# Joins and residuals as accumulating transfers, and two more quarters of attention output by block products

## The chip, the cores and the metric

The kernel runs on one core of a Trainium2 chip. The metric is the device time of one execution in microseconds. TensorE (PE in the profile) multiplies matrices into PSUM. VectorE (DVE), ScalarE (ACT) and GpSimd (POOL) work on SBUF, and DVE and ACT read PSUM too. SyncE (SP) issues most transfers; POOL issues those that add to what is at their destination. Every engine works through its own instructions in the order in which they were written and waits on semaphores.

## The reference

`x` is 2048 tokens of 512 numbers. After a layer norm it goes through attention with 32 heads over a cache of 2048 keys, and through a mixing MLP; the MLP's output, passed through a SiLU, gates the attention's output, and `x` is added.

```python
x = A_x                                           # [1, 2048, 512]
xn = _layernorm(x, axis=-1)
q = (xn @ wq) -> [1, 32, 2048, 128]
p = softmax(q @ k_cache^T * Dh ** -0.5)
s = (p @ v_cache) -> [1, 2048, 4096] @ wo          # attention
g = _silu(_B_ref(xn, w1, w2, w3, w4))              # gate
return x + s * g
```

## The kernel before, in words

**Units and slots.** The 32 heads form eight groups of four (`g` from 0 to 7). The 2048 queries form four quarters of 512 (`qt` from 0 to 3). One head on one quarter is a unit: 128 units, unit number `(g * 4 + qt) * 4 + hh`. A unit takes eight slots of 256 keys. In each slot TensorE makes scores for 256 keys (two matmuls into `ps_s`, L443), ACT takes their exponential (L447), and TensorE multiplies exponentials of ten slots earlier with the values (`ps_o`, L480). The main loop (L1152) writes all other work of all engines into these slots, so its order is fixed by hand: a table `todo` (`at(n, fn)`) and two tables `o_steps` and `o_early` say what is issued in which slot. A slot's number is eight times the unit plus `p`.

**Sums of exponentials.** DVE adds the first two pieces of exponentials (L453) and then the rest; half of one of these adds goes to POOL (`add_half`, L458, at `p == 6`), and DVE's own half and the next add (L462) follow at the start of the next unit. Two folds (L466, L470), a transposing transfer, a reduction (L500), a reciprocal (L506) and two small transfers make the row of factors `rb` with which DVE scales the unit's output into `oT` (L524).

**Queries.** The queries of two heads at a time come from seven block products instead of eight (`product`, L378); DVE puts the pieces together (L424 to L434) just ahead of the unit that needs them. The last of these is L432.

**Output projection.** A quarter of a group, four heads, is multiplied with four heads' rows of `wo`, into `sacc`, one float accumulator per 128 tokens `t` (16 of them). In the plain form (`wo_slot`, `wo_mm`) each `t` takes four matmuls of 512 columns into the bank `xm`, and DVE adds the bank to `sacc` (L668). In the block form (the list `BLOCK`) pairs of token tiles take seven products of two matmuls of 256 columns (`wo_product`, L576), with operand sums on DVE (`wo_sum` L564, `o_sum` L573), and DVE adds partial sums to a tile `sp[qt, i]` of five columns of 256 (`wo_take`, L598). The columns 0 and 2 of it belong to one token tile, 1 and 4 to another, and column 3 holds what has to be added to columns 1, 2 and 4 once, after all groups: this is `wo_join` (L604). The plain quarters of group 7 are then added to the same columns.

**The end.** Token tiles 0 to 7 get their last plain product and are then scaled by half the gate and get `x` added (`y_last`, L674), with `x` and the gate loaded by `fin_load`. For token tiles 8 to 15 (`LATE`) the scaling of `sacc` (`y_scale`, L636) and the addition of `x` (`y_add`, L640, an accumulating transfer that POOL issues) are done ahead of the last product, with the gate loaded by `gate_load` (L607) into buffers that the block form has no more use for. The marker `LATER` (L1109) is the first unit of the quarter behind the last block quarter; joins, scalings and the plan `PLAN` for taking up plain work again are placed relative to it.

Of the kernel before, what the change touches and what calls it, by code (L numbers as in the profile page):

```python
# [9 lines left out]
ALU = mybir.AluOpType  # L10
FP32 = mybir.dt.float32
BF16 = mybir.dt.bfloat16
# [5 lines left out]
def kernel(  # L18
# [15 lines left out]
    nc = tc.nc  # L34
    P = nc.NUM_PARTITIONS

    x2d = A_x.flatten_outer_dims()
    out2d = out.flatten_outer_dims()
    Sq, D = x2d.shape
# [5 lines left out]
    QT = Sq // 512  # L45
# [6 lines left out]
    NG = H // HG  # L52

    SPU = KC // 2
# [7 lines left out]
    pin = tc.keep_in_program_order  # L62

    def pool(name, bufs=1, space=None, **kw):
        if space is not None:
            kw["space"] = space
        return tc.tile_pool(name=name, bufs=bufs, **kw)
# [21 lines left out]
    qtp = ent(pool("qt", 6))  # L89
# [15 lines left out]
    xsrc = x2d.rearrange("(t p) d -> t p d", p=P)  # L105
# [5 lines left out]
    def mm(out, lhsT, rhs, start, stop, **kw):  # L111
# [9 lines left out]
        out=ident[:], in0=diag[:], scalar1=0.0, scalar2=None, op0=ALU.is_equal))  # L121
# [5 lines left out]
    LATE = (QT - 2, QT - 1)  # L127
# [7 lines left out]
    def at(n, fn):  # L135
        todo[n].append(fn)
# [36 lines left out]
    def token(early, name):  # L173
        if early:
            return pL.tile([P, D], BF16, tag="xi", bufs=5, name=name)
        return tokp.tile([P, D], BF16, tag="ta", bufs=6, name=name)
# [21 lines left out]
    gates = {}  # L198
# [337 lines left out]
    def halves(x):  # L536
        return x.rearrange("p (a c) -> p a c", a=2)

    def sa_pair(qt, i):
        x = sp[qt, i] = pS.tile([P, 5, D // 2], FP32, tag="sacc", bufs=NT // 2, name="sacc")  # L540
        sacc[4 * qt + i], sacc[4 * qt + i + 2] = x[:, 0:3:2, :], x[:, 1:5:3, :]
        return x
# [5 lines left out]
    def sa_clear(qt, i):  # L548
        pin(nc.gpsimd.memset(sa_pair(qt, i)[:], 0.0))
# [49 lines left out]

    def wo_join(qt, i):  # L600
        sa = sp[qt, i]
        for out in (sa[:, 2:5:2, :], sa[:, 1:2, :]):
            n = 2 if out is not None and out.shape[1] == 2 else 1
            pin(nc.vector.tensor_tensor(  # L604
                out=out, in0=out, in1=sa[:, 3:4, :].to_broadcast([P, n, D // 2]), op=ALU.add))

    def gate_load(t, i):  # L607
        tag = ("tw0", "so2", "tw3", "so0", "so1", "so3", "tw1", "tw0")[i]
        gin[t] = pS.tile([P, D], BF16, tag=tag, bufs=2 if tag == "tw0" else 1, name="gin")[:]
        pin(nc.sync.dma_start(out=gin[t], in_=gates[t][:]))  # L610

    wog, sp, tw, so, wo_ps, gin = {}, {}, {}, {}, {}, {}
# [12 lines left out]
    fin = {}  # L625

    def fin_load(t):
        xl = token(False, "xl")
        pin(nc.sync.dma_start(out=xl[:], in_=xsrc[t]))
        fin[t] = xl  # L630
        if t // 4 not in LATE:
            gin[t] = token(False, "gl")[:]
            pin(nc.sync.dma_start(out=gin[t], in_=gates[t][:]))

    def y_scale(t):
        pin(nc.vector.scalar_tensor_tensor(  # L636
            out=sacc[t], in0=sacc[t], scalar=0.5, in1=halves(gin[t]), op0=ALU.mult, op1=ALU.mult))

    def y_add(t):
        pin(nc.gpsimd.dma_start(out=sacc[t], in_=halves(xsrc[t]), accum_op=ALU.add))  # L640
# [30 lines left out]

    pair, last = {}, deque()

    def y_last(t):  # L674
        xl, gl = fin.pop(t), gin[t]
        pin(nc.vector.scalar_tensor_tensor(
            out=halves(gl), in0=sacc[t], scalar=0.5, in1=halves(gl), op0=ALU.mult, op1=ALU.mult))
        pin(nc.vector.tensor_tensor(out=xl[:], in0=gl, in1=xl[:], op=ALU.add))
        pin(nc.sync.dma_start(out=out2d[t * P:(t + 1) * P, :], in_=xl[:]))

# [312 lines left out]
    pS = None  # L995
# [57 lines left out]
    def norm_queue(u):  # L1053
        norm(u)
        gg, qq, hh = units[u]
        if hh == HG - 1 and (gg, qq) not in BLOCK:
            wo_todo.extend((gg, 4 * qq + ts) for ts in range(4))
            if gg == NG - 1 and qq not in LATE:
                fin_load(4 * qq)
# [3 lines left out]
    def wo_slot(part, n, each=2, **kw):  # L1063
        gg, t = wo_todo[0]
        if part < HG // each:
            wo_mm(gg, t, tuple(range(part * each, (part + 1) * each)), **kw)
            return
        wo_todo.popleft()
        wo_post(gg, t, n)
        if gg == NG - 1 and t % 4 < 3 and t + 1 not in fin and t // 4 not in LATE:  # L1070
            fin_load(t + 1)

    FIRST, LAST = 14, NU - 4
    BLOCK = [(g, qt) for g in range(NG - 1) for qt in range(QT)][1:-2]
    APART = range(2 * HG, NU - 3)
    pairs = range(FIRST, LAST + 1, 2)
    q_plan = defaultdict(list)
# [2 lines left out]
    for v in pairs:  # L1080
        a = (v - 2) * SPU
# [8 lines left out]
    o_steps, o_early = defaultdict(list), defaultdict(list)  # L1090
    for g, qt in BLOCK:
        u0 = ((g * QT + qt) * HG + 6) * SPU
        for i in range(2):
            a = u0 + 16 * i
# [11 lines left out]
            o_early[u0 + n].append((wo_sum, g, i))  # L1106
    for i, (qt, u) in enumerate((qt, qt * HG + 5 + j) for qt in range(1, QT) for j in range(2)):
        at(u * SPU + 6, lambda qt=qt, i=i: sa_clear(qt, i % 2))
    LATER = (BLOCK[-1][0] * QT + BLOCK[-1][1] + 1) * HG  # L1109
    for u, qt, i in ((-7, 2, 0), (-4, 2, 1), (0, 3, 0), (1, 3, 1), (6, 0, 0), (10, 0, 1), (12, 1, 0), (14, 1, 1)):  # L1110
        o_steps[(LATER + u) * SPU + 3].append((wo_join, qt, i))
    for i, u in enumerate((10, 11, 12, 13, 14, 16, 18, 20)):
        n = (LATER + u) * SPU
        t = 4 * LATE[0] + i
        at(n - 2 * SPU + 4, lambda t=t, i=i: gate_load(t, i))
        at(n + 3, lambda t=t: y_scale(t))
        at(n + 6, lambda t=t: y_add(t))
    CATCH = {2 * HG * SPU + p: x for p, x in {
        0: ((0, "xa"),), 1: ((1, "xa"),), 2: ((2, "xa"),), 3: ((0, "xm"),), 4: ((1, "xm"),),
        5: ((2, "xm"), (0, "xa")), 6: ((1, "xa"),), 7: ((2, "xa"),)}.items()}  # L1120
    PLAN = {2 * HG: (), LATER + 6: (), LATER + 7: ((2, 0), (3, 1), (7, 2)), LATER + 8: ((1, 0), (3, 1), (4, 2), (6, 0), (7, 1)),
            LATER + 9: ((0, 2), (2, 0), (3, 1), (7, 2))}

# [13 lines left out]
    def run_all(plan, n):  # L1137
        for fn, *args in plan.get(n, ()):
            fn(*args)
# [12 lines left out]
    for n in range(UB * SPU):  # L1152
        u, p = divmod(n, SPU)
# [63 lines left out]
            run_all(o_early, n)  # L1217
            add_first(u)
        run_all(o_steps, n)
        if p == 3 and last:  # L1220
            y_last(last.popleft())
        if p == 6:
            add_half(u, nc.gpsimd, LO) if u in APART else add_next(u, 2)
        pay()
# [3 lines left out]
        if pS is None and not held:  # L1228
            right.close()
            pS = right.enter_context(pool("pS", side="right", reuse_waits="tile"))  # L1230
# [7 lines left out]
    n = UB * SPU  # L1238
# [27 lines left out]
    def pv_to(k):  # L1266
# [29 lines left out]
        out=diag[:], in0=diag[:], scalar1=0.0, scalar2=None, op0=ALU.is_equal))  # L1296
# [98 lines left out]
```

## Time and profile before

| | |
|---|---|
| median of three runs | 1221.37 us |
| the three runs | 1220.67 to 1221.55 us |
| the profiled execution | 1220.16 us |
| its span | 1218.4 us |
| granted TensorE clock | 1.000 |
| ACT, exponentials (L447) | 1007.6 us busy |
| DVE, `y_scale` (L636) | 8 of 681 ns |
| moved by transfers | 113.08 MB |

The span runs from the first to the last instruction of the profiled execution; 1.8 us of its time lie around it. Busy shares are averages over stretches that differ: the head of the kernel, until 120 us, is the MLP, and from there to 1198 us the main loop runs. In a line of the timeline stand the start, the length, engine, source line and operation, what is written and read, and in brackets how long the engine was idle before and what it waited for. In a row of stretches stand the stretch, its length, then for each engine the busy time and the number of instructions, the granted clock, the share of the transfer engines and their rate; where only one tile is asked for, only its engine has an entry. In a row of groups stand busy time and the mean of one instruction, and behind the bar the idle time before them.

### The profile page before, as it was taken

How to read it: one execution, taken by the hardware profiler on the slowest of the kernel's cores; microseconds unless marked ns; L12 is line 12 of the kernel's file. 1: busy time of each engine (PE TensorE's matmuls, PEld its weight loads, DVE VectorE, ACT ScalarE, POOL GpSimd, SP SyncE). 2: the span in 40 equal slices, each digit the busy share in tenths (PEclk: the TensorE clock that was granted, in tenths of full speed). 3: DMA queues.
4: the chain of work that ended last, by engine and by line, in shares of the span. 5: the costliest groups of instructions: out<-in, count | busy, mean ns of one | idle time of the engine just before them, and what ended most of it. 6: DMA issues, size and time to landing. Idle time of an engine off the chain costs nothing.

```text
span 1218.4 us, 18896 instructions
## 1 busy us (share of the span) xinstructions
PE 1207.3 (99%) x6556; PEld 676.8 (56%) x6678; DVE 1103.2 (91%) x1945; ACT 1096.6 (90%) x1241; POOL 299.1 (25%) x222
## 2 busy tenths in 40 slices
PE   9999999999999999999999999999999999999998
PEld 7466444555555555555555555555555555555555
DVE  8855789999999999999999999999999999989997
ACT  5444999999999999999999999999999999999996
POOL 5301001323222222222222222222222222233320
PEclk9999999999999999999999999999999999999999
DMA  8771133544334433344343443343344434445542
GB/s 179 176 158 55 40 70 79 96 93 91 82 87 83 104 69 89 83 96 91 75 87 88 99 78 80 87 98 79 85 87 87 105 66 92 84 102 111 122 113 66
DMA packets 248160, 113.08 MB, mean 93 GB/s; under 512 B 195328, under 2 KB 231296, under 8 KB 248064
## 3 DMA queue, kind: packets, MB, share of 16 engines
q1 hardware_dynamic: 244560, 107.21, 40.9%
q0 software_dynamic: 2944, 4.20, 1.5%
q8 instruction: 52, 0.85, 0.3%
q14 instruction: 44, 0.36, 0.2%
q10 hardware_dynamic: 560, 0.46, 0.1%
HBM read 69.60 MB, written 4.45 MB: 61 GB/s over the span
## 4 chain that ended last, share of the span: by engine, by line
PE 98%; issue 1%; ACT 0%; DVE 0%; DVEq 0%; ACTq 0%
PE ps_s L112 41%; PE ps_o L112 38%; PE ps_q L112 8%; PE ps_wo L112 8%; PE ps_m L112 3%; ACT pT L447 0%; PE ps_warm L112 0%; PE ps_oh L112 0%; DVE y L1257 0%; DVE tm L1250 0%; DVE tb L746 0%; PE ps_w L112 0%; DVEq L1390 0%; PE ps_r L112 0%; PE ps_sum L112 0%
## 5 line engine op out<-in xcount | busy, mean ns | idle before, releaser
L447 ACT ACTIVATE pT<-ps_s 128x1024 bf16<-128x1024 f32 x1016 | 1007.6, 1027 | 49.3 <-PE ps_s L112 23.7
L112 PE MATMUL ps_s<-qT,kT 128*128 128x512 bf16 (+1 forms) x2054 | 606.9, 377 | 0.2
L112 PE MATMUL ps_o<-pT,vb 128*128 128x512 bf16 x1885 | 568.7, 379 | 4.7
L458 POOL TENSOR_TENSOR acc<-acc,pT 128x1024 bf16<-128x1024 bf16 x117 | 248.7, 2126 | 728.7 <-ACT pT L447 357.2
L112 PEld LDWEIGHTS <-vb 128*128 128x128 bf16 x1984 | 194.0, 98 | 216.6
L112 PEld LDWEIGHTS <-kT 128*128 128x128 bf16 x2064 | 231.7, 113 | 93.5 <-issue 1.0
L462 DVE TENSOR_TENSOR acc<-acc,pT 128x2048 bf16<-128x2048 bf16 x137 | 167.7, 1224 | 21.1 <-ACT pT L447 5.1
L453 DVE TENSOR_TENSOR acc<-pT 128x2048 bf16<-128x2048 bf16 x127 | 154.8, 1219 | 8.1 <-ACT pT L447 8.0
L598 DVE TENSOR_TENSOR sacc<-ps_wo,sacc 128x512 f32<-128x512 f32 x200 | 123.4, 617 | 14.1 <-PE ps_wo L112 11.2
L466 DVE TENSOR_TENSOR acc<-acc 128x1024 bf16<-128x1024 bf16 x127 | 87.3, 687 | 2.4
L500 DVE TENSOR_REDUCE sm<-tT 128x4 f32<-128x512 bf16 x124 | 84.0, 677 | 5.3 <-DMA tT<-acc 4.9
L524 DVE TENSOR_TENSOR oT<-ps_o,rb 128x512 bf16<-128x512 f32 x127 | 86.5, 681 | 2.2 <-DMA rb<-dr 1.9
L458 DVE TENSOR_TENSOR acc<-acc,pT 128x1024 bf16<-128x1024 bf16 x117 | 79.8, 682 | 0.0
L112 PEld LDWEIGHTS <-wc 128*128 128x128 bf16 x448 | 43.8, 98 | 52.8
L112 PE MATMUL ps_wo<-wo_h,oT 128*128 128x256 bf16 (+1 forms) x295 | 70.7, 307 | 0.2
L112 PEld LDWEIGHTS <-oT 128*128 128x128 bf16 x428 | 41.6, 98 | 45.6
L301 ACT ACTIVATE h2T<-ps_s 128x1024 bf16<-128x1024 f32 x28 | 28.6, 1022 | 35.1 <-PE ps_s L112 35.1
L112 PEld LDWEIGHTS <-so 128*128 128x128 bf16 x400 | 39.1, 98 | 36.5
L470 DVE TENSOR_TENSOR acc<-acc 128x512 bf16<-128x512 bf16 x127 | 54.0, 425 | 4.3
L112 PEld LDWEIGHTS <-wq_h 128*128 128x128 bf16 x396 | 38.7, 98 | 34.3
L112 PE MATMUL ps_q<-xnT,wq_h 128*128 128x256 bf16 (+1 forms) x270 | 55.6, 291 | 0.1
L112 PEld LDWEIGHTS <-w_sb 128*128 128x128 bf16 x368 | 33.6, 98 | 28.9
(136 smaller groups left out, 934.4 us busy)
## 6 DMA issues: line engine op xcount, KB each, us to landing
rb<-dr SPq DMA_DIRECT2D x127, 256.0 KB, 3.8
vb<-in_A_v_cache_dram SPq DMA_DIRECT2D x62, 256.0 KB, 3.0
wq_h<-in_A_wq_dram SPq DMA_DIRECT2D x32, 128.0 KB, 2.5
wo_h<-in_A_wo_dram SPq DMA_DIRECT2D x32, 128.0 KB, 2.3
w_sb<-in_B_w_dram SPq DMA_DIRECT2D x8, 256.0 KB, 4.9
kT<-in_A_k_cache_dram SPq DMA_TRANSPOSE x128, 2.6
gate<-xall POOLq DMA_DIRECT2D x16, 128.0 KB, 2.8
sacc<-in_A_x_dram POOLq DMA_DIRECT2D x8, 256.0 KB, 4.6
```

Source lines behind the costliest of these rows:

```text
L112: pin(nc.tensor.matmul(out=out, lhsT=lhsT, rhs=rhs, start=start, stop=stop, **kw))
L301: pin(nc.scalar.activation(out=h2[c][:, f], in_=ps[:], func=ACT.Gelu_apprx_tanh))
L447: pin(nc.scalar.activation(out=s["pT"][-1][:, jj:jj + 2, :], in_=sps[:], func=ACT.Exp, scale=SCALE))
L453: pin(nc.vector.tensor_tensor(out=s["acc"][:], in0=s["pT"][0][:], in1=s["pT"][1][:], op=ALU.add))
L458: pin(eng.tensor_tensor(out=a[:, part, :], in0=a[:, part, :], in1=e[:, part, :], op=ALU.add))
L462: pin(nc.vector.tensor_tensor(out=a[:], in0=a[:], in1=st[u]["pT"][i][:], op=ALU.add))
L466: pin(nc.vector.tensor_tensor(out=a[:, 0:2, :], in0=a[:, 0:2, :], in1=a[:, 2:4, :], op=ALU.add))
L470: pin(nc.vector.tensor_tensor(out=a[:, 0, :], in0=a[:, 0, :], in1=a[:, 1, :], op=ALU.add))
L500: pin(nc.vector.tensor_reduce(out=sm[:], in_=s["tT"][:], axis=mybir.AxisListType.X, op=ALU.add))
L524: pin(nc.vector.tensor_tensor(out=to, in0=o, in1=rb, op=ALU.mult))
L598: pin(nc.vector.tensor_tensor(out=out, in0=ps, in1=out, op=ALU.add))
```

## The change

The list of block quarters gets the third and fourth quarter of group 6 (before, these were plain), so that `LATER` moves from unit 104 to 112. The joins are no longer two adds by DVE but two accumulating transfers issued by POOL, which read column 3 from SBUF and add it to columns 2 and 4, and to column 1. They stand in units 106, 108, 110, 112, 113, 115, 117 and 119. The scalings of token tiles 8 to 15 stand in units 115 to 122 (before, 114 to 124), the adds of `x` behind them two slots later instead of three, and the gates for them go into other buffers. In `y_last` the residual `x` is no longer loaded by SP and added by DVE, but added to the scaled tile by an accumulating transfer two slots later; the output is issued nine slots later by SP, or, from unit 124 on, three slots later by POOL. One more `y_last` has a place at slot 6 of unit 121.

```diff
     def wo_join(qt, i):
         sa = sp[qt, i]
-        for out in (sa[:, 2:5:2, :], sa[:, 1:2, :]):
-            n = 2 if out is not None and out.shape[1] == 2 else 1
-            pin(nc.vector.tensor_tensor(
-                out=out, in0=out, in1=sa[:, 3:4, :].to_broadcast([P, n, D // 2]), op=ALU.add))
+        for out, n in ((sa[:, 2:5:2, :], 2), (sa[:, 1:2, :], 1)):
+            pin(nc.gpsimd.dma_start(out=out, in_=sa[:, 3:4, :].to_broadcast([P, n, D // 2]), accum_op=ALU.add))

-    def gate_load(t, i):
-        tag = ("tw0", "so2", "tw3", "so0", "so1", "so3", "tw1", "tw0")[i]
-        gin[t] = pS.tile([P, D], BF16, tag=tag, bufs=2 if tag == "tw0" else 1, name="gin")[:]
+    def gate_load(t, tag):
+        pl, n = (qtp, 5) if tag == "qT" else (pS, 2 if tag == "tw0" else 1)
+        gin[t] = pl.tile([P, D], BF16, tag=tag, bufs=n, name="gin")[:]
         pin(nc.sync.dma_start(out=gin[t], in_=gates[t][:]))
...
     def fin_load(t):
-        xl = token(False, "xl")
-        pin(nc.sync.dma_start(out=xl[:], in_=xsrc[t]))
-        fin[t] = xl
-        if t // 4 not in LATE:
-            gin[t] = token(False, "gl")[:]
-            pin(nc.sync.dma_start(out=gin[t], in_=gates[t][:]))
+        fin[t] = gin[t] = token(False, "gl")[:]
+        pin(nc.sync.dma_start(out=gin[t], in_=gates[t][:]))
...
-    def y_last(t):
-        xl, gl = fin.pop(t), gin[t]
+    def y_last(t, n):
+        gl = gin[t]
         pin(nc.vector.scalar_tensor_tensor(
             out=halves(gl), in0=sacc[t], scalar=0.5, in1=halves(gl), op0=ALU.mult, op1=ALU.mult))
-        pin(nc.vector.tensor_tensor(out=xl[:], in0=gl, in1=xl[:], op=ALU.add))
-        pin(nc.sync.dma_start(out=out2d[t * P:(t + 1) * P, :], in_=xl[:]))
+        queue, m = (nc.sync, n + 9) if n < LAST * SPU else (nc.gpsimd, n + 3)
+        at(n + 2, lambda: pin(nc.gpsimd.dma_start(out=gl, in_=xsrc[t], accum_op=ALU.add)))
+        at(m, lambda: pin(queue.dma_start(out=out2d[t * P:(t + 1) * P, :], in_=gl)))
...
-    BLOCK = [(g, qt) for g in range(NG - 1) for qt in range(QT)][1:-2]
+    BLOCK = [(g, qt) for g in range(NG - 1) for qt in range(QT)][1:]
...
+    JOINS = ((-6, 0, 0), (-4, 0, 1), (-2, 1, 0), (0, 1, 1), (1, 2, 0), (3, 2, 1), (5, 3, 0), (7, 3, 1))
+    SCALES = ((8, "tw1", -2, 3), (10, "tw3", -1, 4), (9, "tw0", 0, 5), (11, "qT", 1, 6),
+              (12, "qT", 2, 6), (14, "so2", 5, 7), (13, "so1", 6, 8), (15, "so0", 7, 10))
     LATER = (BLOCK[-1][0] * QT + BLOCK[-1][1] + 1) * HG
-    for u, qt, i in ((-7, 2, 0), (-4, 2, 1), (0, 3, 0), (1, 3, 1), (6, 0, 0), (10, 0, 1), (12, 1, 0), (14, 1, 1)):
+    for u, qt, i in JOINS:
         o_steps[(LATER + u) * SPU + 3].append((wo_join, qt, i))
-    for i, u in enumerate((10, 11, 12, 13, 14, 16, 18, 20)):
-        n = (LATER + u) * SPU
-        t = 4 * LATE[0] + i
-        at(n - 2 * SPU + 4, lambda t=t, i=i: gate_load(t, i))
-        at(n + 3, lambda t=t: y_scale(t))
-        at(n + 6, lambda t=t: y_add(t))
+    for t, tag, a, u in SCALES:
+        at((LATER + a) * SPU + 4, lambda t=t, tag=tag: gate_load(t, tag))
+        at((LATER + u) * SPU + 3, lambda t=t: y_scale(t))
+        at((LATER + u) * SPU + 5, lambda t=t: y_add(t))
...
-        if p == 3 and last:
-            y_last(last.popleft())
+        if (p == 3 or (u, p) == (LATER + 9, 6)) and last:
+            y_last(last.popleft(), n)
```

## Prediction

> **What bounds the kernel now.** I read the page first: span, busy shares, clock, chain.
>
> ```profile
> span 1218.4 us, 18896 instructions
> ...
> PE 1207.3 (99%) x6556; PEld 676.8 (56%) x6678; DVE 1103.2 (91%) x1945; ACT 1096.6 (90%) x1241; POOL 299.1 (25%) x222
> ...
> PEclk9999999999999999999999999999999999999999
> ...
> PE 98%; issue 1%; ACT 0%; DVE 0%; DVEq 0%; ACTq 0%
> ```
>
> The reader is to see that TensorE is busy for 99% of the span at the full clock and that 98% of the chain that ended last is its own work. DVE at 91% is close behind. So time falls only where TensorE gets less to do, and rises only where something makes TensorE wait.
>
> A busy share is an average, so I then took stretches. The first row of each pair below is eight units (98 to 105) in which the output projection runs as block products. The second is eight units (116 to 123) in which it runs as plain products. The first answer is all engines, the second the exponentials alone, the third the projection's matmuls alone.
>
> ```profile
> 950.80:1018.28 67.48, 67.11 (x363) 37.84 (x369) 64.58 (x111) 64.71 (x72) 16.74 (x9) 1.00 0.38 85
> 1104.00:1172.25 68.25, 67.88 (x339) 35.57 (x345) 65.17 (x108) 64.97 (x74) 22.58 (x14) 1.00 0.53 115
> ```
>
> ```profile
> 950.80:1018.28 67.48, 63.48 (x64) 1.00 0.38 85
> 1104.00:1172.25 68.25, 63.70 (x66) 1.00 0.53 115
> ```
>
> ```profile
> 950.80:1018.28 67.48, 10.68 (x56) 1.00 0.38 85
> 1104.00:1172.25 68.25, 12.13 (x32) 1.00 0.53 115
> ```
>
> Both stretches hold the same eight units (64 exponentials; the two more in the second are ones that overlap its edges), and in both TensorE has 0.37 us that is not busy. The block stretch is 0.77 us shorter, with 56 half-width matmuls in place of 32 full ones. What the chain gives for one matmul agrees:
>
> ```profile
> 1151.84 0.43 PE ps_o L112 x2
> 1152.27 0.44 PE ps_q L112 x4
> ```
>
> Two of 512 columns take 0.43 us and four of 256 take 0.44: 0.215 and 0.11 each. A plain quarter has 16 of the former, 3.44 us; a block quarter has 28 of the latter, 3.08 us. That is 0.36 by these rounded rows and 0.77 / 2 = 0.385 by the stretches. I take the stretches, which measure the whole.
>
> **The change part by part.**
>
> *Two more block quarters.* Quarters three and four of group 6 leave the plain form: 2 x 0.385 = 0.77 us less on TensorE, where it is on the path. The marker LATER moves by eight units (104 to 112), and with it the four-unit transition in which plain work restarts; the transition itself keeps its shape, so it is counted at nothing. What is left at the end, units 122 to 127, has the same TensorE work as before.
>
> *DVE's account.* The block form costs DVE more: it reads PSUM eight times and makes four operand sums per quarter.
>
> ```profile
> L598 DVE TENSOR_TENSOR sacc<-ps_wo,sacc 128x512 f32<-128x512 f32 (+1 forms) x16 | 9.8, 613 | 0.8 <-PE ps_wo L112 0.7
> ...
> L604 DVE TENSOR_TENSOR sacc<-sacc 128x512 f32<-128x512 f32 (+1 forms) x6 | 3.1, 551 | 0.0
> ...
> L573 DVE TENSOR_TENSOR so<-oT 128x512 bf16<-128x512 bf16 x4 | 1.5, 416 | 0.0
> ...
> L573 DVE TENSOR_TENSOR so<-so,oT 128x512 bf16<-128x512 bf16 x2 | 0.8, 416 | 0.0
> ```
>
> ```profile
> L668 DVE TENSOR_TENSOR sacc<-ps_wo,sacc 128x512 f32<-128x512 f32 x8 | 5.5, 692 | 1.1 <-PE ps_wo L112 0.8
> ...
> L636 DVE SCALAR_TENSOR_TENSOR sacc<-sacc,gin 128x512 f32<-128x512 f32 x5 | 3.4, 682 | 0.0
> ...
> L678 DVE TENSOR_TENSOR xl<-gl,xl 128x512 bf16<-128x512 bf16 x5 | 2.1, 426 | 0.2
> ```
>
> Per quarter 8 x 0.613 + 4 x 0.416 = 6.57 us, against 4 x 0.692 = 2.77 plain: 3.8 more, 7.6 for two quarters. Gone are the 16 join adds (8 pairs of 0.551 each way, 8.8 us) and eight residual adds (8 x 0.426 = 3.4 us). DVE ends 4.6 us lighter. On TensorE that is worth nothing, since TensorE did not wait for it: relief on a covered engine stays covered.
>
> *The eight scalings.* They move from units 114 to 124 to units 115 to 122, five of them in units 115 to 119, which are now block stage. Here a local overload of DVE can stop TensorE. The nearest thing seen is units 104 and 105, each with one join pair (1.02 us) in the block stage:
>
> ```profile
> 1005.71 1.02 DVE L604 TENSOR_TENSOR sacc<-sacc 128x512 f32<-128x512 f32 x2
> 1006.65 1.22 DVE L453 TENSOR_TENSOR acc<-pT 128x2048 bf16<-128x2048 bf16 x1
> 1007.78 0.69 DVE L598 TENSOR_TENSOR sacc<-ps_wo,sacc 128x512 f32<-128x512 f32 x1
> ...
> 1010.10 0.68 DVE L458 TENSOR_TENSOR acc<-acc,pT 128x1024 bf16<-128x1024 bf16 x1
> ```
>
> ```profile
> 1008.74 0.38 PE L112 MATMUL ps_wo<-wo_h,so 128*128 128x256 bf16 x2
> ```
>
> ```profile
> 1016.45 0.68 DVE L432 TENSOR_TENSOR qT<-ps_q,tq 128x512 bf16<-128x512 f32 x1
> ```
>
> ```profile
> 1017.61 0.59 PE L112 MATMUL ps_s<-qT,kT 128*128 128x512 bf16 x2
> ```
>
> The PSUM read at 1007.78 ends at 1008.47 and the next product into that bank starts at 1008.74: 0.27 us to spare. One unit later the new queries are ready at 1017.13 and wanted at 1017.61: 0.48 to spare. So 1.02 + 0.42 us of extras ahead of the PSUM read (join and one operand sum) still fit. Unit 116 gets a scaling and a sum (0.68 + 0.42), unit 118 two scalings and no sum, as no further block quarter follows (1.36): each less than the 1.44 that fitted. Units 117 and 119 get 0.68 each, less than the 1.02 of unit 105. Cost taken: 0. If DVE enters unit 118 half a microsecond late, the spare of 0.27 + 0.08 is gone and TensorE waits some 0.2 us; the bound is 0 to 1.5 us for the five together (0.3 each). A gain is excluded: nothing waits there now. Units 120 to 122 carry scalings, final scalings and PSUM reads together, but there each product has two slots (2.2 us) behind it.
>
> *Joins as accumulating transfers.* Sixteen issues on POOL, in units 106, 108, 110, 112, 113, 115, 117 and 119; then eight residual transfers and three output transfers there. POOL's rows around its half of the accumulator add, and for the transfers that it issues already:
>
> ```profile
> 1008.00 2.12 POOL L458 TENSOR_TENSOR acc<-acc,pT 128x1024 bf16<-128x1024 bf16 x1 [6.97 <-ACT qT L416]
> 1016.67 2.13 POOL L458 TENSOR_TENSOR acc<-acc,pT 128x1024 bf16<-128x1024 bf16 x1 [6.55 <-ACT pT L447]
> ```
>
> ```profile
> L640 POOL DMA_DIRECT2D sacc<-in_A_x_dram x8: 1061/1080/1156, 1095.7 to 1181.1; - x8
> ...
> DMA to landing us min/median/max: 3.5/4.6/4.8
> ```
>
> ```profile
> L321 POOL DMA_DIRECT2D gate<-xall x16: 539/539/787, 78.5 to 189.3; - x16
> ```
>
> A two-row-block transfer costs POOL 1.08 us, a one-block transfer 0.54: a join pair 1.62 us, in a hole of 6.55. All eight joins (13 us), the eight adds of x (8.6, as before) and the residuals (4.3) lie in such holes. What queues behind them on POOL is its half add, and DVE's half waits for that: at 1010.10 it starts as POOL's ends (1008.00 + 2.12). So a late POOL shows at once. The add of x is now issued ahead of POOL's half instead of behind it. POOL's half needs DVE's L453 anyway, which comes after the scaling in DVE's order and takes 1.13 us from start to the next start (1006.65 to 1007.78): it covers the 1.08. In unit 118 two adds take 2.16; the second scaling and L453 cover 0.6 + 1.13 of it, leaving some 0.4 late, once. I take 0.
>
> No row shows an accumulate from SBUF to SBUF. Its landing I bound by 2.4 us (128 KB loads) and 6.0 us, and take 4.6 from the nearest row, which accumulates into the same tile.
>
> ```profile
> xl<-in_A_x_dram SPq DMA_DIRECT2D x8, 128.0 KB, 2.4
> ...
> w_sb<-in_B_w_dram SPq DMA_DIRECT2D x1, 512.0 KB, 6.0
> ```
>
> The first reader is a scaling, one unit (8.4 us) behind for the last two joins and two or more for the others. Covered at either bound.
>
> The page "SBUF — State Buffer" of the Trainium skill (section "SBUF: two separate sides") speaks against this part: while DVE runs an operation in its two-port mode, descriptors issued from GpSimd cannot be written and the transfer starves. By that rule the issues would stretch to whatever DVE leaves free; the eight issues above, at 1061 to 1156 ns beside a DVE that is 95% busy, show none of it.
>
> *SP's queue* loses eight loads of x. Its outputs stand seven slots (7.4 us) behind the issue of the add of x that they wait for, which takes 4.6 us to land, so SP does not stand in front of the sums' transfers. The gate loads into other buffers wait for block operands last read 1 to 8 slots earlier: 0.
>
> **Sum.** 1220.16 us is the profiled execution's time, span 1218.4 and 1.8 around it. Less 0.77 gives 1219.4. The median of the three runs, 1221.37, is 1.21 above the profiled execution; the forecast for a median is 1221.37 - 0.77 = 1220.6, that is -0.06%. A measurement of this kernel tells about 0.2% (2.4 us) from no change, so this is within it.
>
> **Rivals.**
>
> *DVE's spare runs out* in units 115 to 121. For it: spares of 0.27 and 0.48 us, and 64.58 of 67.48 us busy. Against it: the new extras are smaller than those that fitted. Price 0.3 us in three to five units: 1221.5 to 1222. The gain is eaten, no more.
>
> *POOL is held by the joins* (slower). If the second transfer of a pair has to wait for the first to land, POOL is held from the end of its last half add, 1010.12, for 4.6 + 0.54 us, until 1015.3; its next half starts at 1016.67. It decides when a landing takes over 6 us. Each further microsecond delays DVE's half in eight units, with 0.3 to 0.5 us of spare each: at 7 us, 8 x 0.6 = 5 us, or 1225.5; at 8 us, 1233. For it: the new transfers share the engines with 0.38 to 0.53 of other traffic. Against it: landings of 4.8 at most.
>
> *Issues starved on POOL*: 1.62 us would have to grow fourfold to fill the hole of 6.55. At fivefold, 8.1, the half is 1.5 us late in eight units, about 9 us: 1230. The issue rows, 1.16 us at most, give it little. It is the rule of the Trainium skill's page named above, as a mechanism of this kernel.
>
> *Faster than the sum*: TensorE's idle in the stretches is 0.37 in 68 us, so DVE's relief has at most some 1 us to win back between unit 98 and the end: 1219.6. Beyond 2.4 us there is no room.
>
> **Chances.** The forecast with no new wait, 1219.9 to 1221.3: 0.58. DVE's spare used up, 1221.3 to 1223: 0.14. POOL held, 1224 to 1233: 0.13. Issues starved: 0.03. A wait that I do not see, above 1224: 0.06. More than the sum: 0.06, nearly all of it still within 0.2%; I leave 0.05 for faster by over 0.2%. Slower by over 0.2% is the POOL cases and little else, 0.22; the rest, 0.73, is no change. The range takes the first two cases and the beginning of the third: 1219.6 to 1224.0.
>
> **What will show it.** Right: a stretch of eight units 110 to 117 of 67.5 us with 64 exponentials; TensorE's chain share 98%; POOL's issues of joins near 1.08 and 0.54 us; DVE half adds starting right as POOL's end. Wrong: waits of TensorE behind L598 or L432 in units 115 to 121; POOL's half starting over 0.5 us behind L453's end; scalings on DVE idle for a DMA; landings of joins over 6 us.

## The result, and the profile after

The changed kernel takes 1223.07 us (median of 15 runs, 1222.44 to 1224.86) beside 1220.51 us for the kernel before (15 runs on the same chip, 1219.99 to 1221.55). The ratio is 1.0023, with a 95% interval of 1.0016 to 1.0031. It is slower by 2.6 us; the forecast was 1220.6 us, no change. The base of that forecast, 1221.37, was a median of three runs; from the median of 15 the same sum gives 1220.51 - 0.77 = 1219.7 us.

The profiled execution of the changed kernel took 1223.71 us, 3.55 more than the one before. From its page, the span, the engines and the chain that ended last:

```profile
span 1221.9 us, 18969 instructions
...
PE 1206.9 (99%) x6580; PEld 678.2 (56%) x6702; DVE 1102.5 (90%) x1937; ACT 1096.5 (90%) x1241; POOL 325.9 (27%) x249
...
PE 93%; DVE 4%; DMA 1%; ACT 1%; issue 1%; SPq 0%; POOL 0%; DVEq 0%; ACTq 0%
```

TensorE's work has become less (1206.9 for 1207.3 us), and so has DVE's (1102.5 for 1103.2 us), both by less than the forecast 0.77 and 4.6 us. But the chain, which was 98% TensorE, now has 4% of DVE and 1% of transfers in it: something new is waited for.

The next two answers cut the end of the main loop into units 110 to 117, 118 and 119, and 120 to 123, first before, then after. The columns are the stretch, its length, each engine's busy time with its instructions, the clock, the share of the transfer engines and their rate.

```profile
1052.03:1121.04 69.01, 68.64 (x345) 36.19 (x351) 61.81 (x105) 64.62 (x73) 20.38 (x12) 1.00 0.49 106
1121.04:1138.11 17.07, 17.02 (x87) 8.88 (x87) 16.31 (x28) 16.25 (x20) 5.83 (x4) 1.00 0.59 123
1138.11:1172.24 34.13, 33.92 (x170) 17.80 (x173) 32.91 (x55) 32.49 (x37) 10.47 (x7) 1.00 0.52 117
```

```profile
1052.94:1120.42 67.48, 67.11 (x363) 37.81 (x369) 63.55 (x111) 64.50 (x73) 30.72 (x21) 1.00 0.69 135
1120.42:1137.39 16.97, 16.86 (x88) 9.14 (x89) 16.32 (x27) 15.96 (x19) 9.33 (x7) 1.00 0.78 118
1137.39:1174.66 37.27, 35.46 (x174) 18.05 (x176) 34.38 (x52) 32.89 (x38) 14.69 (x12) 1.00 0.55 114
```

The eight units 110 to 117 take the 67.5 us that were forecast. Against the kernel before that is 1.53 us less, and the transition into plain work, which now lies in units 119 to 122, takes part of that back. The rest of the loop is decided in units 120 to 123: 3.14 us longer than before. Of the 37.27 us TensorE is idle for 1.81 (37.27 - 35.46), against 0.21 before. The share of the transfer engines in units 110 to 119 has risen from 0.49 and 0.59 to 0.69 and 0.78.

The 3.5 us by which the span grew are thus: 0.91 ahead of the first exponential, where nothing was changed and where the executions of this study differ by up to 1.2 us; 0.00 from there to unit 110; -1.53, -0.10 and +3.14 in the three stretches; and 1.1 behind unit 123, which the last section comes to.

What TensorE waited for between 960 and 1200 us (waiter, what it waited for, us in total, times, longest); for the kernel before the list is empty:

```profile
PE ps_q L112 <- DVE qT L429: 0.7, 1, 0.7
PE ps_wo L112 <- DVE sacc L662: 0.4, 1, 0.4
PE ps_q L112 <- DVE tq L424: 0.4, 1, 0.4
```

And what DVE waited for; before, no transfer was in this list:

```profile
DVE sm L500 <- DMA tT<-acc: 3.1, 5, 1.4
DVE sacc L598 <- PE ps_wo L112: 2.4, 11, 0.3
DVE oT L524 <- DMA rb<-dr: 1.0, 2, 0.7
```

Three late results of DVE, then, and, ahead of them on DVE, waits for the two transfers of the softmax sums: the transposing one (`tT`) and the one that brings the factors (`rb`). The timeline of DVE shows three places at which it lost most:

```profile
1136.51 0.68 DVE L524 TENSOR_TENSOR oT<-ps_o,rb 128x512 bf16<-128x512 f32 x1
1138.59 0.69 DVE L500 TENSOR_REDUCE sm<-tT 128x4 f32<-128x512 bf16 x1 [1.41 <-DMA tT<-acc]
...
1153.90 0.68 DVE L432 TENSOR_TENSOR qT<-ps_q,tq 128x512 bf16<-128x512 f32 x1
1154.50 2.29 DVE L670 SCALAR_TENSOR_TENSOR gl<-sacc,gl 128x512 bf16<-128x512 f32 x1
...
1166.94 1.51 DVE L458 TENSOR_TENSOR acc<-acc,pT 128x1024 bf16<-128x1024 bf16 x1
```

First, 1.41 us idle for `tT` at the start of unit 120. Second, the final scaling that was put at slot 6 of unit 121: 2.29 us, where its seven sisters take 0.68. Third, a half add (L458) of 1.51 instead of some 0.7 us. The second and third are not idle time but long instructions, so no list of waits shows them. POOL's timeline says what goes on beside them:

```profile
1129.98 2.16 POOL L603 DMA_DIRECT2D sacc<-sacc  x2
...
1154.12 2.12 POOL L458 TENSOR_TENSOR acc<-acc,pT 128x1024 bf16<-128x1024 bf16 x1
...
1163.74 1.08 POOL L634 DMA_DIRECT2D sacc<-in_A_x_dram  x1 [5.78 <-DVE sacc L630]
1164.46 1.28 POOL L673 DMA_DIRECT2D gl<-in_A_x_dram  x1
1165.04 2.85 POOL L458 TENSOR_TENSOR acc<-acc,pT 128x1024 bf16<-128x1024 bf16 x1
```

The scaling begins at 1154.50, inside POOL's half add (1154.12 to 1156.24), and ends at 1156.79, 0.55 us after it: it stood until POOL was done. In unit 122 two issues (L634 and L673) push POOL's half to 1165.04 to 1167.89, and DVE's own half, begun at 1166.94, ends 0.56 us behind that. Both pairs read two operands from SBUF on DVE while POOL reads SBUF. The Trainium skill has this as a rule (page "SBUF — State Buffer", section "Who interferes with whom"): a DVE instruction with two SBUF inputs shares a port pair with a GpSimd instruction that reads SBUF, and the one that comes second stands still until the other has ended. The trace agrees, at 2.29 for 0.68 us. In the kernel before no such pair overlapped by more than 0.33 us.

The joins themselves, from the answer on the line that issues them (first row: duration of one issue, minimum, median and maximum in ns):

```profile
L603 POOL DMA_DIRECT2D sacc<-sacc x16: 1203/1324/1425, 1018.4 to 1130.7; - x16
...
DMA to landing us min/median/max: 3.8/5.4/7.3
```

The `tT` that DVE waited for at the start of unit 120 was under way beside the pair issued at 1129.98: the pair landed at 1136.28 and 1138.05, `tT` at 1138.57. In the chain that ended last (start, length, what), this late transfer and the held scaling stand one behind the other, with TensorE, ACT and DVE in turn between them:

```profile
1133.35 5.22 DMA tT<-acc
1138.59 0.70 DVE sm L500
...
1154.58 2.21 DVE gl L670
```

### The profile page after: what moved, and what is told of

The parts are those of the page before. It is cut to its first block, busy times and chain, and to the rows that moved or that the text cites. A ratio compares the mean times of both kernels' runs of the same rounds, so it can differ in the third digit from the quotient of the medians.

```text
span 1221.9 us, 18969 instructions
## 1 busy us (share of the span) xinstructions
PE 1206.9 (99%) x6580; PEld 678.2 (56%) x6702; DVE 1102.5 (90%) x1937; ACT 1096.5 (90%) x1241; POOL 325.9 (27%) x249
## 4 chain that ended last, share of the span: by engine, by line
PE 93%; DVE 4%; DMA 1%; ACT 1%; issue 1%; SPq 0%; POOL 0%; DVEq 0%; ACTq 0%
PE ps_s L112 39%; PE ps_o L112 36%; PE ps_wo L112 8%; PE ps_q L112 7%; PE ps_m L112 3%; ACT pT L447 1%; DVE bn L205 1%; DMA xin<-in_A_x_dram 1%; DVE acc L462 1%; DMA tT<-acc 0%; DMA w_sb<-in_B_w_dram 0%; DVE gl L670 0%; DVE acc L466 0%; PE ps_oh L112 0%; DVE xall L226 0%
## 5 line engine op out<-in xcount | busy, mean ns | idle before, releaser
L458 POOL TENSOR_TENSOR acc<-acc,pT 128x1024 bf16<-128x1024 bf16 x117 | 250.8, 2144 | 659.7 <-DVE acc L453 371.6
L453 DVE TENSOR_TENSOR acc<-pT 128x2048 bf16<-128x2048 bf16 x127 | 154.7, 1218 | 7.0 <-ACT pT L447 6.7
L598 DVE TENSOR_TENSOR sacc<-ps_wo,sacc 128x512 f32<-128x512 f32 x216 | 133.4, 617 | 16.7 <-PE ps_wo L112 13.6
L458 DVE TENSOR_TENSOR acc<-acc,pT 128x1024 bf16<-128x1024 bf16 x117 | 81.2, 694 | 0.0
L112 PEld LDWEIGHTS <-so 128*128 128x128 bf16 x432 | 42.3, 98 | 39.5
L112 PE MATMUL ps_wo<-wo_h,oT 128*128 128x256 bf16 (+1 forms) x279 | 61.7, 297 | 0.6 <-DVE sacc L662 0.4
```

What stands on the lines that cost most here:

```text
L112: pin(nc.tensor.matmul(out=out, lhsT=lhsT, rhs=rhs, start=start, stop=stop, **kw))
L453: pin(nc.vector.tensor_tensor(out=s["acc"][:], in0=s["pT"][0][:], in1=s["pT"][1][:], op=ALU.add))
L458: pin(eng.tensor_tensor(out=a[:, part, :], in0=a[:, part, :], in1=e[:, part, :], op=ALU.add))
L598: pin(nc.vector.tensor_tensor(out=out, in0=ps, in1=out, op=ALU.add))
```

## The experiments

Times are medians, each with the ratio to the kernel before on the same chip and its 95% interval. Two theories were at stake. The first: the joins' transfers crowd the transfer engines, the sums' transfers land late, and DVE idles. The second: the final scaling in unit 121 stands behind POOL's half add.

**The final scaling moved** from unit 121 to 125:

```diff
-        if (p == 3 or (u, p) == (LATER + 9, 6)) and last:
+        if (p == 3 or (u, p) == (LATER + 13, 6)) and last:
```

> The changed kernel with one edit: the extra final scaling at slot 6 of unit 121 goes to slot 6 of unit 125, where POOL has no half add. Theory 'port' (that scaling reads two SBUF operands while POOL adds, and is held 1.6 us; everything behind it on DVE is late): the waits of TensorE at 122.1, 122.5 and 123.5 (0.30 + 0.54 + 0.87 us) go for the most part, 1221.4 to 1221.8 us. Theory 'transfers' (the joins' transfers slow the transposing transfer of the sums, DVE idles 1.4 and 0.5 us in units 119 and 120, and all later waits come from there): nothing changes, 1222.7 us or more.

Measured: 1223.42 us, 1.0020 (1.0012 to 1.0029). The long scaling is gone (all eight now within 660 to 684 ns), and so are TensorE's waits in units 122 and 123; the time is not better. POOL's half in unit 122 is still pushed back by its two issues, and DVE's half add behind it still takes 1.60 us. The profiled execution waits elsewhere, in units 115 to 120. What DVE and then TensorE waited for in it:

```profile
DVE sm L500 <- DMA tT<-acc: 6.2, 7, 1.7
...
DVE oT L524 <- DMA rb<-dr: 1.7, 2, 1.2
```

```profile
PE ps_wo L112 <- DVE sacc L598: 0.8, 1, 0.8
PE ps_wo L112 <- DVE sacc L662: 0.6, 1, 0.6
PE ps_s L112 <- DVE qT L432: 0.2, 1, 0.2
```

Up to unit 121 the two kernels issue the same work, and yet TensorE waited there in this execution and hardly in the other; between 960 and 1197 us DVE lost 7.9 us to the two transfers here and 4.1 there. What the sums' transfers cost varies from one execution to the next. So the second theory alone does not carry the loss.

**The joins left out**, all else as in the change:

```diff
-            pin(nc.gpsimd.dma_start(out=out, in_=sa[:, 3:4, :].to_broadcast([P, n, D // 2]), accum_op=ALU.add))
+            pass
```

> The changed kernel without any join: the addition of column 3 to columns 1, 2 and 4 is left out, and so are its sixteen transfers. Theory 'transfers': DVE's idle time ahead of the reductions in units 119 and 120 goes, and with it the waits of TensorE, 1221.0 us or less. Theory 'port': only the wait at 120.6 (0.60 us) can go, the scaling in unit 121 is still held, 1222.4 us. If neither, it stays at 1223.

Measured: 1222.16 us, 1.0010 (1.0001 to 1.0019). `tT` makes DVE wait no more (`rb` still does once, 1.0 us); the scaling in unit 121 is still held (1682 ns), the half add two units later takes 1.95 us, and TensorE waits once for L429, 0.7 us. Units 120 to 123:

```profile
1136.77:1172.59 35.82, 34.98 (x174) 18.06 (x176) 34.07 (x52) 32.50 (x38) 14.51 (x12) 1.00 0.61 114
```

**Both: joins left out and the scaling moved.**

> Both single edits at once: no joins (left out, with their transfers) and the extra final scaling at slot 6 of unit 125. If the two causes seen so far are all there is (waits for transfers that the joins slow, and the scaling held by POOL's half add), no wait of TensorE is left from unit 98 to 127, the stretch of units 96 to 126 takes 262.9 us (before the change 263.6), and the time is 1219.6 to 1220.0 us. If DVE's load in these units is too much as such, waits of over 0.5 us remain and it is 1220.6 or more.

Measured: 1220.56 us, 1.0000 (0.9991 to 1.0009). The three stretches of it, to be held against those of before and after:

```profile
1052.81:1120.29 67.48, 67.11 (x363) 37.83 (x369) 63.78 (x113) 64.49 (x73) 20.07 (x11) 1.00 0.52 108
1120.29:1137.25 16.96, 16.85 (x88) 9.12 (x89) 16.56 (x27) 15.95 (x18) 7.72 (x6) 1.00 0.60 100
1137.25:1172.23 34.98, 34.82 (x174) 18.14 (x176) 32.16 (x52) 32.50 (x38) 14.37 (x11) 1.00 0.59 111
```

Their sum is 119.42 us, 0.79 below the 120.21 of before: this is the 0.77 that was forecast for the two block quarters. The medians do not show this gain: 1220.56 us beside 1220.66 for the kernel before on the same chip, and the interval reaches 0.09% to either side. TensorE is idle for 0.64 us in all of it, as before, and waits for nothing. It also gives the price of each of the two causes alone. With the joins out, the held scaling costs 35.82 - 34.98 = 0.84 us in units 120 to 123; by the medians it is 1222.16 - 1220.56 = 1.6, with intervals that overlap. With the scaling moved, the whole joins cost 1223.42 - 1220.56 = 2.9 us, with intervals that do not. The two do not add up (the changed kernel has both, and its median is 2.5 above this one): why moving the scaling gains nothing as long as the joins are whole was not settled.

How the joins cost can be read from the landings. Eight transposing transfers `tT` overlap a join in the changed kernel. They land with a median of 3.8 us there and 4.0 with the scaling moved; the same eight take 2.7 and 2.6 in the two kernels without joins. For the eight `rb` that overlap a join there is no such difference: 4.0 and 4.2 us with joins, 4.3 and 3.9 without. So the traces show the joins slowing `tT`, and do not show them slowing `rb`. `tT` is issued at once in all of them (a median of 0.03 us behind DVE's last fold), so SP's queue does not hold it up.

**Joins at half their transfers**: the scaling moved, and of each join only the transfer to column 1 (128 KB); columns 2 and 4 are left without it.

```diff
-        for out, n in ((sa[:, 2:5:2, :], 2), (sa[:, 1:2, :], 1)):
+        for out, n in ((sa[:, 1:2, :], 1),):
```

> The run with the scaling moved, with only the smaller transfer of each join (column 1; the addition to columns 2 and 4 is left out): 8 transfers of 128 KB instead of 16 that carry 384 KB per join. If it is the volume of the joins on the transfer engines that lengthens the sums' transfers, the time lies between the run without joins (1220.56) and the one with all (1223.42), nearer to the former: 1221.0 to 1222.0, and the transposing transfer's median landing in units 106 to 119 between 2.7 and 3.6 us. If a join costs by its wait or its issue alone, whatever its size: 1223.

Measured: 1220.33 us, 0.9999 (0.9990 to 1.0008). The three stretches sum to 119.42 us again:

```profile
1052.18:1119.66 67.48, 67.11 (x363) 37.82 (x369) 63.65 (x112) 64.51 (x73) 23.77 (x16) 1.00 0.60 115
1119.66:1136.63 16.97, 16.86 (x88) 9.15 (x89) 16.38 (x27) 15.96 (x19) 8.58 (x7) 1.00 0.74 119
1136.63:1171.60 34.97, 34.81 (x174) 18.10 (x176) 32.54 (x52) 32.51 (x38) 14.43 (x11) 1.00 0.64 111
```

The share of the transfer engines is 0.74 in units 118 and 119, nearly the 0.78 of the changed kernel: the mean share is not what decides. The joins' rows:

```profile
L603 POOL DMA_DIRECT2D sacc<-sacc x8: 857/885/1533, 1017.7 to 1128.4; - x8
...
DMA to landing us min/median/max: 2.7/2.9/3.8
```

One transfer of 128 KB by itself lands in 2.9 us. In the changed kernel, right behind the one of 256 KB, the same transfer has a median of 5.6 us. Eight single ones cost nothing that shows.

**A join's two transfers in two units**: complete, the scaling moved, the second transfer one unit behind the first.

```diff
-        o_steps[(LATER + u) * SPU + 3].append((wo_join, qt, i))
+        for part in range(2):
+            o_steps[(LATER + u + part) * SPU + 3].append((wo_join, qt, i, part))
```

> The run with the scaling moved, complete, with the two transfers of each join in two units, one behind the other, instead of both in one. If the burst of both at once is what meets the sums' transfers, waits get shorter and it is 1221 to 1222.5; if the volume over the stretch counts, 1223.4 as with both in one.

Measured: 1220.95 us, 1.0003 (0.9994 to 1.0012), 2.5 us better than with the pairs whole. Landings fall to 2.7 to 6.4 us. Its profiled execution, at 1222.11 us the slowest of its eleven, still has waits of TensorE (1.0 us in all) behind a wait of DVE for `rb` of 1.6 and one for `tT` of 1.1 us. Bytes, issues and readers are those of the whole pairs, so neither the volume nor the joins' own readers explain the 2.5 us. The traces speak against POOL being held too: in the changed kernel POOL's half starts 0.15 us at most behind the end of L453 in every unit from 99 to 124 but unit 122, where it is 0.46. What differs is when the second transfer is in flight: never beside the first of its own join. DVE waits for `tT` 3.1 to 8.4 us in the five kernels of this study that have whole pairs at the new places, 1.4 us here, and 0 to 0.4 us where the joins are halved or left out.

**The joins alone as transfers**, in the kernel before, at their old places and with the old blocks:

```diff
-            pin(nc.vector.tensor_tensor(
-                out=out, in0=out, in1=sa[:, 3:4, :].to_broadcast([P, n, D // 2]), op=ALU.add))
+            pin(nc.gpsimd.dma_start(out=out, in_=sa[:, 3:4, :].to_broadcast([P, n, D // 2]), accum_op=ALU.add))
```

> The kernel before with the joins alone as transfers (residuals and all else as before). If the joins are what cost in the run with the transfers alone (1222.46), this is the same, 1222 to 1222.8; if it was the residuals or the outputs behind them, it is as before, 1220.3 to 1221.0.

Measured: 1221.81 us, 1.0010 (1.0001 to 1.0019). DVE is relieved of the 8.8 us of joins, and the kernel is slower by 1.1. The waits of DVE in it, then units 118 and 119, which took 17.07 us before, and the piece of the chain that makes them longer:

```profile
DVE oT L524 <- DMA rb<-dr: 3.2, 5, 1.1
DVE sm L500 <- DMA tT<-acc: 2.8, 3, 1.6
```

```profile
1122.24:1140.35 18.11, 17.36 (x87) 8.81 (x87) 15.28 (x26) 16.36 (x19) 8.45 (x7) 1.00 0.65 137
```

```profile
1126.55 5.66 DMA tT<-acc
```

Here too a `tT` came late beside a pair of joins (landed at 1130.90 and 1131.69, `tT` at 1132.21), and TensorE waited for L429 and L432 behind it.

**Joins and residuals as transfers**, in the kernel before, at the old places and with the old blocks: the same edit, and `fin_load` and `y_last` as in the change.

> The kernel before with the transfers alone: joins and residuals as accumulating transfers at the places of before, block quarters and scalings as before. The transfers slow the sums' transfers here too, but these units have plain work, with longer spares, and no scaling in POOL's window: same as before within 0.5 us, 1220.1 to 1221.1. If the transfers cost by themselves, without a crowded DVE: 1222 or more.

Measured: 1222.46 us, 1.0015 (1.0006 to 1.0024). DVE waits for `rb` 3.6 us and for `tT` 2.6 us in all, none above 1.0, and in the profiled execution TensorE waits for none of it: three stretches of 120.21 us, as before, in an execution of 1221.66 us. So the transfers make the kernel slower by themselves, without block quarters and without the scaling in unit 121, but this trace does not show where: it has the waits on DVE, and all of them still fit. Whether the residuals add to the joins' price stays open: the two medians, 1222.46 and 1221.81, have intervals that overlap.

**The opposite**: the new places and the two block quarters, but joins and residuals on DVE as before, with `x` loaded by SP.

```diff
-            pin(nc.gpsimd.dma_start(out=out, in_=sa[:, 3:4, :].to_broadcast([P, n, D // 2]), accum_op=ALU.add))
+            pin(nc.vector.tensor_tensor(
+                out=out, in0=out, in1=sa[:, 3:4, :].to_broadcast([P, n, D // 2]), op=ALU.add))
```

> The two more block quarters and all the new places, but joins and residuals on DVE as before the change, no new transfers. If the transfers are what costs: faster than the changed kernel, 1221 to 1222, though DVE has 1.02 us more in each join unit and 0.43 more per final scaling. If DVE's load in units 119 to 123 as such is what costs, whatever the transfers do: slower than the changed kernel, 1224 or more.

Measured: 1225.74 us, 1.0042 (1.0028 to 1.0056). Its units 110 to 117:

```profile
1053.38:1123.74 70.36, 68.26 (x363) 37.66 (x369) 67.39 (x121) 64.75 (x73) 19.61 (x12) 1.00 0.46 104
```

DVE is busy for 67.39 of 70.36 us and TensorE is idle for 2.10. At the new places the block quarters need DVE's relief: without it these units take 70.36 instead of 67.48 us. Units 120 to 123 take 37.31 us, as in the change, since the scaling in unit 121 is held here too (2290 ns). Of the two prices the transfers' is the smaller.

**POOL's order**: the add of `x` behind POOL's half again, and the residual and its output two slots later.

```diff
-        queue, m = (nc.sync, n + 9) if n < LAST * SPU else (nc.gpsimd, n + 3)
-        at(n + 2, lambda: pin(nc.gpsimd.dma_start(out=gl, in_=xsrc[t], accum_op=ALU.add)))
+        queue, a, m = (nc.sync, n + 4, n + 11) if n < LAST * SPU else (nc.gpsimd, n + 2, n + 3)
+        at(a, lambda: pin(nc.gpsimd.dma_start(out=gl, in_=xsrc[t], accum_op=ALU.add)))
...
-        at((LATER + u) * SPU + 5, lambda t=t: y_add(t))
+        at((LATER + u) * SPU + 6, lambda t=t: y_add(t))
```

> The changed kernel with POOL's issues put behind its half add: the adds of x to the accumulators at slot 6 (as before the change) instead of 5, the residual of the final scalings four slots behind instead of two, their outputs eleven instead of nine. Theory 'order' (two issues ahead of the half add in units 120 and 122 make it late and hold DVE's half, 0.8 us in unit 123): the half adds of POOL start as DVE's first add ends, and 0.5 to 0.9 us come back, 1222.2 to 1222.6. Theories 'port' and 'transfers': no change, 1223.

Measured: 1225.95 us, 1.0042 (1.0030 to 1.0055), slower than the change. The scaling in unit 121 is held as before (2292 ns), and `tT` takes up to 8.0 us to land. From the answer on the tile `tT` between 960 and 1197 us, here and then in the kernel before:

```profile
DMA to landing us min/median/max: 2.4/3.6/8.0
```

```profile
DMA to landing us min/median/max: 2.4/2.9/4.1
```

The edit does what it was made for: no half add of DVE takes over 683 ns any more. But the pair of joins in unit 119 lands after 8.7 and 9.3 us, DVE waits 8.4 us in all for `tT`, and the time rises. So the order of POOL's issues against its half is not what decides.

**The last join later**: the scaling moved, the last join from unit 119 to 123, and the two scalings that read it to units 124 and 126.

```diff
-    JOINS = (... (5, 3, 0), (7, 3, 1))
+    JOINS = (... (5, 3, 0), (11, 3, 1))
```

> The changed kernel, complete, with the last join (quarter 3, second pair) in unit 123 instead of 119, the scalings of token tiles 13 and 15 in units 124 and 126 instead of 120 and 122, and the extra final scaling at slot 6 of unit 125. Theory 'transfers and port': the wait of DVE in unit 119 (1.4 us) and the held scaling go, waits in units 115 to 118 may stay, 1220.0 to 1221.5 us. If the times of the joins do not matter: 1223.

Measured: 1222.97 us, 1.0018 (1.0009 to 1.0027). TensorE's wait in unit 120 is gone; the one in unit 118 (0.8 us) stays, behind the join of unit 117. One join fewer in the crowd is not enough.

**The scalings spread** over units 115 to 126, with the last join in unit 123 as in the run above and the extra final scaling at slot 2 of unit 122:

```diff
-    SCALES = ((8, "tw1", -2, 3), (10, "tw3", -1, 4), ...
+    SCALES = ((8, "tw1", -2, 3), (10, "tw3", -1, 5), (9, "tw0", 0, 7), (11, "qT", 1, 12),
+              (12, "qT", 2, 7), (14, "so2", 5, 12), (13, "so1", 6, 13), (15, "so0", 7, 14))
```

> As the run with the late join, but the scalings thinner over units 115 to 119 (115, 117 and two in 119, the other four in 124 to 126), and the extra final scaling at slot 2 of unit 122, ahead of POOL's half add. If what hurts is a wait for a transfer together with a scaling in the same unit, the waits in units 115 to 118 go too: 1219.8 to 1220.6 us. If DVE's load moves the trouble to units 122 to 126: 1221.5 or more.

Measured: 1223.98 us, 1.0028 (1.0017 to 1.0039). The stretch 120 to 123 is free of waits (34.98 us), but later units pay: DVE's half add in unit 125 takes 2.49 us beside POOL's half, and TensorE waits in units 125 and 127, 0.6 us each. Room made in one place was taken from another.

**The kernel before once more**, for the spread between its own executions.

> The kernel before once more, for a second profile: how far the head (120.7 us to the first exponential), the tail (20.79 us behind unit 126) and the landings of the sums' transfers differ between two executions of one program. If the changed kernel's longer head (121.6) and tail (21.95) come from the change, this shows 120.7 and 20.8 again; if they vary by themselves, within 1 us of them.

Measured: 1220.26 us. `tT` has a median of 3.3 us and a maximum of 3.8 in units 106 to 119, against 2.9 and 4.1 in the first execution, and the loop from unit 96 to 126 takes 254.91 us against 254.92. Landings vary without joins too, but not so far that DVE waits for `tT`; for `rb` it waits 0.6 us in all.

## Why the prediction was wrong, point by point

The forecast was a gain of 0.77 us; the kernel became 2.6 us slower. That 1223.07 lies within the stated range of 1219.6 to 1224.0 owes something to luck. The range was drawn for DVE's spares running out in units 115 to 121 and for the mildest case of POOL being held; the wait that came, for `tT`, stands in no rival, and "a wait that I do not see" was priced above 1224.

*Two more block quarters, 0.77 us less on TensorE, the transition counted at nothing*: right. The kernels without waits measure 0.79. The stretch that was named came out at 67.48 us with 64 exponentials.

*DVE lighter, worth nothing on TensorE*: right in sign. Of the 4.6 us, 3.6 show with the scaling moved (1099.6 us busy beside 1103.2) and 0.7 in the changed kernel, where DVE's instructions stand beside POOL's. And the opposite experiment shows that the relief was not idle: without it units 110 to 117 take 2.9 us more.

*"Cost taken: 0" for the eight scalings*, by the spares of 0.27 and 0.48 us: in units 115 to 119 right by the kernels with half joins or none, in which TensorE waits for nothing there. The spares decide all the same, since they are what a transfer that lands late has to use up.

*"Units 120 to 122 carry scalings, final scalings and PSUM reads together, but there each product has two slots (2.2 us) behind it"*: this step failed. It counted DVE's instructions at their usual length. The additional final scaling stands in the time of POOL's half add and takes 2.29 for 0.68 us. The waits came in units 120 to 123, for L662, L424 and L429, and not, as the prediction had it, for L598 and L432 in units 115 to 121; in the kernel with the scaling moved those two waits did come (0.8 and 0.2 us). With the joins out, this costs 0.84 us of the loop and 1.6 us of the median (by intervals that overlap). "DVE's half waits for that", said of POOL's half, was the same thing misread: DVE's half begins before POOL's ends (1166.94 and 1167.89) and stands inside the instruction.

*Joins as transfers*: the step with most of the error. Issues of "1.08" and "0.54" us were taken from transfers out of other tensors; the joins took 1.20 to 1.43 us each, whether of one or two columns, and the residuals 0.87 for 0.54. That by itself cost little, since POOL had the hole. The landing was bounded at 6.0 us and taken at 4.6, and measured 3.8 to 7.3 us. "Covered at either bound" held for the joins' own reader: no scaling waited for a transfer. What the sum left out is who else uses the transfer engines. DVE's reduction stands behind the transposing transfer of the sums in each unit, `tT` lands later when a pair of joins is in flight (a median of 3.8 instead of 2.7 us for the same eight), and this term of the sum, put at nothing because it was not asked, measures 2.9 us with the scaling moved and 1.1 in the old kernel.

*The rivals*: "POOL is held by the joins" has the right condition (landings beyond 6 us) and the wrong mechanism. The second transfer of a pair is issued without waiting for the first (two issues in 2.16 us), and POOL's half was not held by a landing: it starts 0.15 us at most behind L453 in every join unit. Starved issues are not seen: a pair of joins was issued in 2.16 us for the 1.62 taken, not in four times as much. "A wait that I do not see" is what came, at a lower price than the one given for it.

*SP's queue*: right, no wait of SP in front of these outputs (L674) shows.

What stays open is why the two causes do not add, and whether a placement of the joins exists in which they are all complete and never beside `tT` or `rb`. POOL issues a join as soon as its half and the semaphores allow, in five of the eight pairs of the changed kernel right behind the half, so the slot it was written in sets its time only loosely. None of the complete kernels was faster than the kernel before; the one with split joins equals it within its interval.

## What to carry to other kernels

A transfer that replaces work of a covered engine can be paid for by other transfers in flight at that moment, as `tT` was here: before moving work to the transfer engines, list which short transfers the critical engine waits behind, and issue the new ones singly (here one of 128 KB cost nothing, pairs of 256 and 128 KB cost 1 to 3 us, and the same pairs split over two units nothing beyond the noise). When an operation is moved, look at what runs on POOL at its new place, and not only at how much room DVE has: an operation with two SBUF operands stood here until POOL's add was done. A gain of 0.06% rests on all others staying as they are, so price the neighbours before the gain.

## What the runs showed of the hardware that was not expected

An accumulating transfer from SBUF to SBUF of 128 KB took 2.7 to 3.8 us alone (one of eight in the split kernel took 5.4) and a median of 5.6 us right behind one of 256 KB, and POOL was busy for 0.86 to 2.2 us with issuing one join transfer of either size.

A load of instructions goes with a late last output. In the profiled execution of the changed kernel the last output landed 2.72 us after its issue (1218.13 to 1220.85), in the one before 1.75 us. The transfers of the last 3 us, after:

```profile
q14 instruction: 1, 0.01, 1.4%
issues: line engine op xcount, KB each, median us to landing
out_dram<-y SPq DMA_DIRECT2D x2, 64.0 KB, 2.1
```

And from 1215.6 us on, before:

```profile
q10 hardware_dynamic: 144, 0.07, 12.1%
issues: line engine op xcount, KB each, median us to landing
out_dram<-y SPq DMA_DIRECT2D x2, 64.0 KB, 1.6
```

After, an instruction load of 8 KB ran in that time (1.4% of 16 engines over 3 us is 0.67 us on one of them); before, none. The executions of the kernel with the scaling moved, of the one with spread scalings and of the one with the late join show a load there too, with the last output landing in 2.73, 2.88 and 2.05 us; in the ten others no load falls into that time, and it lands in 1.74 to 1.76. This is 1 us of the 3.5 between the two profiled executions, though not of the loop. It goes with the load in the traces; no run isolates it.
